# A segmented attention block: the second K product by column halves, half sums of token rows on GpSimd, and a new order of the work

## The chip, the cores and the metric

The kernel runs on one core of a Trainium2 chip. The metric is the device time of one execution in microseconds (us). The kernel before took 807.91 us, the median of three runs (808.39, 807.91 and 807.34).

## The reference

The input x has 2048 tokens of 512 columns. They are cut into 64 segments of 32 tokens, and the segments form a chain: the first eight output rows of one segment, its memory rows, stand ahead of the tokens of the next.

```
h = x + attention(layernorm(x));  out = h + mlp(layernorm(h))

attention: 32 heads of width 128
mem = mem0                                   # 8 rows
for s in range(64):
    h = concatenate([mem, x[32*s : 32*s+32]])   # 40 rows
    q, k, v = h @ Wq, h @ Wk, h @ Wv            # 512 -> 32 heads x 128
    p = softmax(where(mask, q k^T * scale, -1e9))
    o = (p v) @ Wo
    mem = o[:8];  outs.append(o[8:])
mask: a memory row sees all 40 rows; a token sees the memory, itself and the tokens before it
mlp: layernorm, 512 -> 1792, gelu, 1792 -> 512, with biases
```

All weights are bf16. Two layernorms follow one another ahead of the mlp.

## The kernel before

**Packs.** A segment's eight memory rows are on the chain; its tokens are not. The kernel works on 32 rows at a time: pack A of segment s holds its 8 memory rows and 24 of its token rows (tile hT, a ring of slots). The other 8 token rows of four segments are pack B of a block (tile hB), worked one block ahead. There are 16 blocks `bk` of four segments; `sg` = s % 4 is the place of a segment in its block.

**Passes.** A product of a pack with half of WK, WQ or WV (16 heads, 2048 columns) is four passes, one per 128 rows of the weights (`passes` L857, `one_pass` L880). A pass is four matmuls side by side in the columns of TensorE, each 128 rows by 32 columns, streaming 512 columns of weights. `hT` is the stationary operand. A matmul whose stationary operand is still loaded may leave out the load (L605); others load it (L872). K0, K1, Q0, Q1, V0 and V1 are the six products of pack A. Those of pack B, four passes each, fill gaps and are called F0 and F1: eight F passes in each segment of blocks 1 to 14. In sg 3 they are instead the WO product of pack B.

**One segment on TensorE.** Its order is written by hand in ORDERS (L37), one list for each sg: the passes of Q and K, then SC0 (scores of the memory rows and of pack B's rows for heads 0 to 15, L1037, 16 matmuls), V passes and F passes with SC1 (heads 16 to 31) among them, PV0 (probabilities times V of the first half, L1075 and L1080), PVA (L1143, token rows of the segment before), one F pass, the first quarter of WO (L1171, 16 matmuls), PV1, the rest of WO (48 matmuls), SA (scores of pack A's token rows, L1105), and F passes. The next segment then waits for the memory rows in hT.

**The other engines.** The chain of a segment passes through them. K and Q: ScalarE (ACT) or VectorE (DVE) copies the product out of PSUM (L890, L891 with the scale, into tile kq), DVE turns it (L913, into KALL and QT), and GpSimd (POOL) spreads the queries (L927, into ZC). Scores: DVE takes the maximum (L1045, nmc), ACT two exponentials (L1054, EC with its sum smc), DVE for each a reciprocal (L1059, rsc) and a normalized copy (L1062, PC), then one turning (L1064, PTC) that PV waits for. Result: ACT copies PV's output (L890, OT; OTm0 and OTm1 below are its memory rows of PV0 and PV1), WO follows, DVE turns its whole result (L1183, TT), and adds its two halves for the memory rows (L1177, hT, two adds). For the token rows DVE adds the halves likewise (L1177, opT, two adds of 64x96), in its own time. V is copied by ACT (L890, VS; VS0 and VS1 for the halves). GpSimd makes the probabilities of token rows (L1126, PA; turned by DVE L1128) and spreads them (L1132, BD) for PVA, and folds pack B's WO result (L1223 to L1227). The attention's result of a block is turned back by a transposing DMA (`nat`, L1239) and added to x.

**What sets the order.** All operations are recorded with the tiles that they read and write. A planner (`schedule`, L236) then places those that aren't TensorE's: a table PLAN (L43) gives each kind a time within its segment, HOME (L100) the engine where several can do it; an operation goes into the first gap on its engine's line that is free at its earliest time. BANK (L42) gives each product its PSUM bank. Waits on semaphores follow from reads and writes. The order of each engine's queue is fixed by this when the program is built.

After the attention, the mlp runs in its own phase.

## Time and profile before

| what | value |
|---|---|
| median of three runs | 807.91 us |
| span of the profiled execution | 805.9 us (2.05 less than that median) |
| TensorE (PE) busy | 775.0 us, 96% |
| VectorE (DVE) busy | 621.0 us, 77% |
| ScalarE (ACT) busy | 527.1 us, 65% |
| GpSimd (POOL) busy | 349.6 us, 43% |
| a block of four segments, in the middle | 41.14 us |

A row of the timeline gives the start of an instruction (or of several alike) in us from the start of the span, its length in us, its engine, its line in the kernel, the operation, output and inputs by the program's names, shapes and a count. Brackets show idle time ahead of it and what ended that. PEld is TensorE's load of weights, which overlaps the matmuls. TensorE's ends are modelled, so a distance is read from start to start. A row of the waits gives the engine and line that waited, what it waited for, the total in us, the times, and the longest.

### The profile page before, as it was taken

The page shows a single profiled execution, that of the slowest core. Times are in us where ns is not written, and L with a number is a line of the kernel's source. Part 1 is how long each engine was busy: PE and PEld are TensorE (multiplying, and loading weights), DVE is VectorE, ACT ScalarE, POOL GpSimd, SP SyncE. Part 2 cuts the span into 40 slices and gives each one's busy share as a digit, 9 for nine tenths or more (in the row PEclk, how much of TensorE's full clock was granted, in tenths as well). Part 3 has the DMA queues.
Part 4 walks back from the last instruction along what each step waited for, and adds up shares of the span by engine and source line. Part 5 has one row for each costly group of instructions (what it writes and reads, how often), then busy time and mean ns, then how long its engine had stood idle before and what let it go on. Part 6 is the DMA issues. An engine that isn't in the chain of part 4 may idle for free.

```text
span 805.9 us, 43594 instructions
## 1 busy us (share of the span) xinstructions
PE 775.0 (96%) x19308; PEld 422.5 (52%) x18891; DVE 621.0 (77%) x2008; ACT 527.1 (65%) x1522; POOL 349.6 (43%) x886
## 2 busy tenths in 40 slices
...
DMA packets 65449, 48.03 MB, mean 60 GB/s; under 512 B 29028, under 2 KB 61676, under 8 KB 65260
## 3 DMA queue, kind: packets, MB, share of 16 engines
...
q10 hardware_dynamic: 332, 0.27, 0.1%
...
## 4 chain that ended last, share of the span: by engine, by line
PE 91%; DVE 3%; DMA 2%; SPq 2%; ACT 1%; issue 1%; POOL 0%
PE ps L872 43%; PE ps L1171 16%; PE ps L605 6%; PE quad L1579 6%; PE ps L1572 5%; PE ps L1210 4%; PE quad L1075 3%; DMA WQ<-in_A_Wq_dram 2%; SPq L775 2%; PE ps L1105 2%; PE quad L1037 2%; PE ps L1365 2%; PE quad L1143 1%; PE quad L1080 1%; DVE PC L1062 1%; ACT kq L890 1%
## 5 line engine op out<-in xcount | busy, mean ns | idle before, releaser
L872 PE MATMUL ps<-WQ,hT 128*32 128x512 bf16 x2048 | 157.4, 382 | 3.4 <-DVE hT L1177 3.3
L1171 PE MATMUL ps<-WO,OT 128*32 128x256 bf16 x4224 | 140.8, 275 | 1.0 <-ACT OT L890 1.0
L872 PE MATMUL ps<-WV,hT 128*32 128x512 bf16 x1780 | 138.7, 379 | 0.0
L891 ACT ACTIVATE kq<-ps 128x512 bf16<-128x512 f32 x146 | 87.2, 597 | 63.7 <-PE ps L872 63.4
L1126 POOL TENSOR_TENSOR PA<-SA,rsa 128x256 bf16<-128x256 f32 x64 | 39.9, 624 | 183.0 <-DVE rsa L1119 170.6
L890 ACT CAST kq<-ps 128x512 bf16<-128x512 f32 x160 | 93.4, 584 | 38.2 <-PE ps L872 38.2
L1171 PEld LDWEIGHTS ps<-WO,OT 128*32 128x32 bf16 x4224 | 96.2, 97 | 26.5 <-ACT OT L890 12.3
L1132 POOL COPY BD<-PTA 32x192 bf16<-32x192 bf16 x256 | 95.5, 373 | 16.6 <-DVE PTA L1128 0.8
L1062 DVE SCALAR_TENSOR_TENSOR PC<-EC,rsc,even 128x128 bf16<-128x128 f32 x256 | 94.5, 370 | 6.7
L872 PE MATMUL ps<-WK,hT 128*32 128x512 bf16 x1292 | 92.5, 379 | 0.0
L872 PEld LDWEIGHTS ps<-WQ,hT 128*32 128x32 bf16 x2048 | 57.0, 96 | 57.9 <-issue 18.7
L913 DVE STREAM_TRANSPOSE KALL<-kq 128x256 f32<-128x256 f32 x160 | 70.5, 440 | 20.8 <-ACT kq L890 18.6
L1054 ACT ACTIVATE EC<-quad,nmc 128x64 f32<-128x64 f32 x252 | 77.1, 311 | 5.9 <-DVE nmc L1045 0.2
L605 PE MATMUL ps<-WK,hT 128*32 128x512 bf16 x756 | 74.6, 379 | 0.0
L890 ACT CAST VS<-ps 128x512 bf16<-128x512 f32 x126 | 73.7, 585 | 0.7
L890 ACT CAST OT<-quad 128x128 bf16<-128x128 f32 (+1 forms) x205 | 66.3, 363 | 7.5 <-PE quad L1080 5.7
L913 DVE STREAM_TRANSPOSE QT<-kq 128x256 f32<-128x256 f32 x128 | 57.0, 445 | 15.5 <-ACT kq L891 14.1
L872 PEld LDWEIGHTS ps<-WV,hT 128*32 128x32 bf16 x1780 | 50.5, 96 | 34.2 <-issue 1.0
L1575 ACT ACTIVATE WQ<-ps,b1t 128x512 bf16<-128x512 f32 x42 | 28.9, 688 | 52.0 <-PE ps L1572 52.0
L872 PEld LDWEIGHTS ps<-WK,hT 128*32 128x32 bf16 x1292 | 36.4, 97 | 46.1 <-issue 20.1
L1117 ACT ACTIVATE SA<-SA 128x256 f32<-128x256 f32 x64 | 26.7, 417 | 49.4 <-DVE SA L1116 45.0
L1223 POOL TENSOR_TENSOR opT<-TTB,TTS 32x64 bf16<-32x64 f32 x128 | 40.3, 315 | 31.7 <-DVE opT L1177 22.5
...
## 6 DMA issues: line engine op xcount, KB each, us to landing
...
```

The lines of the kernel that those rows point to most:

```text
L605: return e.add_instruction(mybir.InstMatmult(name="I-%d" % (4000000 + _kept[0]), engine=mybir.EngineType.PE, start_tensor_calc=start, stop ...
L872: ins = e.matmul(o, l, m, start=(k == 0), stop=(k == DC - 1), tile_position=(0, 32 * j), skip_group_check=True)
L890: return {"act": (lambda e: e.copy(out, src), t_act(n, ps_)), "dve": (lambda e: e.tensor_copy(out, src), 0.155 + 1.0e-3 * n * fast)}
L891: return {"act": (lambda e: e.mul(out, src, scale_), t_act(n, ps_)), "dve": (lambda e: e.tensor_scalar(out, src, scale_, None, ALU.mult), ...
L913: S.op("dve", lambda e: e.transpose(out, src), reads=[("kq", i)], writes=[key], dur=t_dve(256) + 0.02)
L1054: return e.activation(EC[:, r, sl, :], o[:, sl, :], ACTF.Exp, bias=nmc[:, r, sl:sl + 1], accum_out=smc[:, r, sl:sl + 1])
L1062: S.op("dve", lambda e, sl=sl, xc=xc: e.scalar_tensor_tensor(PC[:, r, :, :, sl], xc, rsc[:, r, sl:sl + 1], ev, ALU.mult, ALU.mult), reads= ...
L1132: S.narrow(S.op("pool", lambda e, j=j, rows=rows: e.tensor_copy(BD[rows, par, :, j, :, :], PTA[rows, :, 0:NA, :]), reads=["PTA"], writes=[ ...
L1171: ins = e.matmul(ps[bank][32 * j:32 * j + 32, 0:256], lhs(slot(h)), wo_cols(h, b), start=(k == 0), stop=(k == 15), tile_position=(0, 32 * ...
L1223: return e.tensor_tensor(o[32 * q:32 * q + 32, c:c + 2], x, y, ALU.add)
L1572: ins = e.matmul(ps[bank][:, 0:SBT], W1[:, cc, fc * P:(fc + 1) * P], hnT_of(k)[:, cc, :], start=(cc == 0), stop=(cc == DC - 1))
L1579: S.op("pe", lambda e: e.matmul(quad[:, t, :], gT_of(k, fc)[:, t * P:(t + 1) * P], W2[:, fc, :], start=(fc == 0), stop=(fc == FC - 1)), re ...
```

## The change

**K1 by column halves.** For every segment but the first, the second K product is done in two halves of its columns, each into a bank of its own (K1 and KX): eight half passes of four matmuls with 256 columns. Their sequence is KSEQ, pairs of half and weight row block; the first half is whole after six of the eight. Each half has its own copy (kql, then kq), its own turning (KAl, then KA, 128x128), its own group of scores (SC1 of 8 matmuls, and SC2), its own prefill of the mask, and its own maximum (nmc, nmd). The exponentials wait for their own maximum.

**Token rows' half sums.** Flag OPA moves the two opT adds from DVE to GpSimd: a copy of the lower halves of TT (opS, 64x192), then two adds (64x96). `nat` waits for both.

**WO's result.** The new code can turn and add it in two halves (TT2); the flag is off, so it is turned and added whole.

**Order.** ORDERS, BANK, PLAN and HOME are new; PLAN has a number for each sg. The planner keeps planned operations on an engine in the order in which they come to it (`placed`). K0 comes ahead of Q0, and pairs of K and Q passes share a loaded operand (3228 matmuls use a kept load, 1024 before). The flags PVM, NRM and P3 are off.

TensorE in segment 37 (sg 1), from the first scores to PV0. L1037 are the scores, `WV,hT` V passes, `WQ,hB` F passes, L1075 PV0. Before:

```order
L1037 MATMUL quad<-KALL,ZC 32x64 x16
L872 MATMUL ps<-WV,hT 32x512 x4
L605 MATMUL ps<-WV,hT 32x512 x4
L872 MATMUL ps<-WV,hT 32x512 x12
L872 MATMUL ps<-WQ,hB 32x512 x4
L1037 MATMUL quad<-KALL,ZC 32x64 x16
L872 MATMUL ps<-WQ,hB 32x512 x4
L872 MATMUL ps<-WV,hT 32x512 x12
L872 MATMUL ps<-WQ,hB 32x512 x4
L1075 MATMUL quad<-PTC,VS 128x2x16 x8
```

The same place now, from the second V pass on (ahead of it stand the 16 matmuls of SC0 and one V pass); L1107 are the scores, L913 and L638 the passes, L1216 PV0:

```order
L638 MATMUL banks<-WV,hT 32x512 x4
L913 MATMUL banks<-WV,hT 32x512 x4
L638 MATMUL banks<-WV,hT 32x512 x4
L1107 MATMUL banks<-KALL,ZC 32x64 x8
L913 MATMUL banks<-WQ,hB 32x512 x4
L913 MATMUL banks<-WV,hT 32x512 x4
L638 MATMUL banks<-WV,hT 32x512 x4
L1107 MATMUL banks<-KALL,ZC 32x64 x8
L913 MATMUL banks<-WV,hT 32x512 x4
L638 MATMUL banks<-WV,hT 32x512 x4
L913 MATMUL banks<-WQ,hB 32x512 x12
L1216 MATMUL banks<-PTC,VS 128x2x16 x8
```

SC1 stood behind six passes; now its first half stands behind four and its second half behind seven. Four F passes stand ahead of PV0 instead of three; behind WO there are three instead of four. In the other sg three F passes stand ahead of PV0 as before, all of them behind SC2.

DVE in segment 39 (sg 3), from the turning of Q1 to the second softmax's turning. L1045 are the maxima, L1059 the reciprocals, L1062 the normalized copies, L1064 the turnings. Before:

```order
L913 STREAM_TRANSPOSE QT<-kq 128x256
L1045 TENSOR_REDUCE nmc<-quad 128x2
L913 STREAM_TRANSPOSE KALL<-kq 128x256
L1059 RECIPROCAL rsc<-smc 128x1
L1062 SCALAR_TENSOR_TENSOR PC<-EC,rsc,even 128x128
L1059 RECIPROCAL rsc<-smc 128x1
L1045 TENSOR_REDUCE nmc<-quad 128x2
L1062 SCALAR_TENSOR_TENSOR PC<-EC,rsc,even 128x128
L1064 STREAM_TRANSPOSE PTC<-PC 128x128
```

Now (L1118 is the whole maximum, L1124 the half ones, PC0 and PTC0 belong to the first softmax, PC1 and PTC1 to the second):

```order
L973 STREAM_TRANSPOSE QT<-kq 128x256
L1118 TENSOR_REDUCE nmc<-banks 128x2
L987 STREAM_TRANSPOSE KALL<-kq 128x4x32 x2
L1124 TENSOR_REDUCE nmc<-banks 128x1
L1156 RECIPROCAL rsc<-smc 128x1 x2
L1159 SCALAR_TENSOR_TENSOR PC0<-EC,rsc,even 128x128 x2
L1156 RECIPROCAL rsc<-smc 128x1
L1124 TENSOR_REDUCE nmc<-banks 128x1
L1161 STREAM_TRANSPOSE PTC0<-PC0 128x128
L1159 SCALAR_TENSOR_TENSOR PC1<-EC,rsc,even 128x128
L1156 RECIPROCAL rsc<-smc 128x1
```

Ahead of PTC0 there are now two half turnings for one whole one, and two half maxima for one whole one; in this sg a reciprocal of the second softmax stands there too. In sg 0 and 2 one reciprocal precedes the half maximum, in sg 0 the other half maximum stands between the two PCs, and in sg 2 the turning of PA stands between the two half turnings.

ACT in segment 38 (sg 2), from the first exponential to the copy of PV0's memory rows (`OT`). Before:

```order
L1054 ACTIVATE EC,smc<-quad,nmc 128x64 [waits sem_dve]
L1054 ACTIVATE EC,smc<-quad,nmc 128x64
L890 CAST VS<-ps 128x512 [waits sem_pe]
L1054 ACTIVATE EC,smc<-quad,nmc 128x64 [waits sem_dve]
L1054 ACTIVATE EC,smc<-quad,nmc 128x64
L890 CAST VS<-ps 128x512 [waits sem_pe]
L890 CAST OT<-quad 128x2x8x8 [waits sem_pe]
```

Now:

```order
L1127 ACTIVATE EC,smc<-banks,nmc 128x64 [waits sem_dve]
L1127 ACTIVATE EC,smc<-banks,nmc 128x64
L1127 ACTIVATE EC,smc<-banks,nmc 128x64 [waits sem_dve]
L950 CAST VS<-banks 128x512 [waits sem_pe]
L1127 ACTIVATE EC,smc<-banks,nmc 128x64 [waits sem_dve]
L950 CAST OT<-banks 128x2x8x8 [waits sem_pe]
L950 CAST VS<-banks 128x512
```

The second V copy stood ahead of the copy of PV0's rows and stands behind it now.

The diff, cut to its core (of ORDERS the list of sg 1, of PLAN two lines):

```diff
-PHASE = (0, 64, 128, 192)
+PHASE = (113, 177, 241, 49)
+TT2, SPL, KCOL, PVM, NRM, P3 = False, True, True, False, 0, False
+OPA = True
+AHEAD = 2.1
+KSEQ = ((0, 0), (1, 0), (1, 1), (0, 1), (0, 2), (0, 3), (1, 3), (1, 2))
...
-          (('Q0', 0, 1), ('K0', 0, 1), ('Q0', 1, 2), ('K0', 1, 2), ('Q0', 2, 3), ('Q1', 0, 1), ('Q0', 3, 4), ('K0', 2, 4), ('Q1', 1, 4), ('K1', 0, 4), ('SC0', 0, 99), ('V0', 0, 1), ('V1', 0, 1), ('V0', 1, 4), ('F1', 0, 1), ('SC1', 0, 99), ('F1', 1, 2), ('V1', 1, 4), ('F1', 2, 3), ('PV0', 0, 99), ('PVA', 0, 99), ('F1', 3, 4), ('WO', 0, 2), ('PV1', 0, 99), ('WO', 2, 8), ('SA', 0, 99), ('F0', 0, 4)),
+          (('K0', 0, 1), ('Q0', 0, 2), ('K0', 1, 2), ('Q0', 2, 3), ('K0', 2, 3), ('Q0', 3, 4), ('K0', 3, 4), ('Q1', 0, 2), ('K1', 0, 1), ('Q1', 2, 4), ('K1', 1, 8), ('SC0', 0, 99), ('V1', 0, 1), ('V0', 0, 2), ('V1', 1, 2), ('SC1', 0, 99), ('F1', 0, 1), ('V1', 2, 3), ('V0', 2, 3), ('SC2', 0, 99), ('V0', 3, 4), ('V1', 3, 4), ('F0', 0, 1), ('F1', 1, 3), ('PV0', 0, 99), ('PVA', 0, 99), ('F1', 3, 4), ('WO', 0, 2), ('PV1', 0, 99), ('WO', 2, 8), ('F0', 1, 3), ('SA', 0, 99), ('F0', 3, 4)),
...
-        "PTC0": (5.74,) * 4,
+        "PTC0": (5.468, 5.559, 5.632, 5.541),
-        "VS1": (6.72,) * 4,
+        "VS1": (7.186, 7.51, 6.962, 7.039),
...
+            fixed = planned(o) is not None
...
-                i = bisect.bisect_right(ST, t)
+                i = max(bisect.bisect_right(ST, t), placed[eng] + 1 if fixed else 0)
...
+        def half_passes(lhs, reads, slot, W, key, r, banks):
+            for n, (h, cc) in enumerate(KSEQ):
+                pad = [0, False]
+                ks = [c for g, c in KSEQ if g == h]
...
+                    for j in range(4):
+                        w = W[:, cc, r * 2048:(r + 1) * 2048].rearrange("p (a y b e) -> p y a b e", a=4, y=2, b=2)[:, h, :, :, 32 * j:32 * j + 32]
+                        o, l, m = ps[banks[h]][32 * j:32 * j + 32, 0:256], lhs(cc), w
...
         def k_seg(s, r, bank):
             par, a0 = s % 2, (s % 2) * HP + 8 * r
+            if r == 1 and SPL and s > 0:
+                for h, (a, b) in enumerate((("kql", "KAl"), ("kq", "KA"))):
...
+                    S.either(copy2(half, v, 256), reads=[("ps", bh)], writes=[(a, r)])
...
-        def sc_softmax(s, r, bank):
+        def sc_softmax(s, r, banks):
...
+                if not whole:
+                    S.op("dve", lambda e, sl=sl, o=o: e.tensor_reduce(nmc[:, r, sl:sl + 1], o[:, sl, :], AX.X, ALU.max, negate=True), reads=[bkey], writes=[("nmd" if sl else "nmc", r)], dur=0.22)
...
+                x = S.op("act", ex, reads=[("nmc" if whole or sl == 0 else "nmd", r)] + [bkey] * (sl or not whole), writes=[ek, sk], dur=0.37)
...
+                    if OPA:
+                        v = TTSX[64:128].rearrange("p c q t -> p (c q t)")[:, 0:2 * DC * NA].rearrange("p (c q t) -> p c q t", c=DC, q=2)
+                        S.narrow(S.op("pool", lambda e: e.tensor_copy(v, tt[0:64, :, :, 0:NA]), reads=[("TTl", par)] * TT2 + [("TT", par)], writes=["opS"], dur=0.35, after=after))
+                        for q2 in range(2):
+                            S.narrow(S.op("pool", lambda e, q2=q2: e.tensor_tensor(o[64 * q2:64 * q2 + 64], tt[64:128, :, q2, 0:NA], v[:, :, q2], ALU.add),
+                                          reads=["opS", ("TT", par)] + [("TTl", par)] * TT2, writes=[("opA%d" % q2, (sx // 4) % 2, sx % 4)], dur=0.4, after=after))
...
+                    if name == "SC1" and SPL and s > 0:
+                        for n_, half in (("SC1", 0), ("SC2", 1)):
...
+                            sc_mm(s, 1, bank_of[n_], half)
...
```

426 lines of the change are left out of this document (286 added, 140 removed), and 4 rows, old and new, of the table ORDERS.

## The prediction

> **What bounds the kernel now.** I read the page's head first, then the windows by block of four segments, the waits by what ended last, and the timelines of one segment. Engines are named as in the profile.
>
> ```profile
> span 805.9 us, 43594 instructions
> PE 775.0 (96%) x19308; PEld 422.5 (52%) x18891; DVE 621.0 (77%) x2008; ACT 527.1 (65%) x1522; POOL 349.6 (43%) x886
> ```
> ```profile
> 410.90:452.04 41.14, 41.14 (x1172) 23.03 (x1117) 37.08 (x124) 30.08 (x91) 20.22 (x52) 1.00 0.13 29
> ```
>
> The span is 805.9 and the median of the runs 807.9, so 2.05 us lie around the span. PE looks full: busy for all of the 41.14 us of a block (10.285 a segment), at the full granted clock. But its ends are modelled and matmuls overlap. The waits (engine, line, what it waited for: total us, times, longest) show that it does wait:
>
> ```profile
> PEld L870 <- DVE hT L1177: 24.8, 62, 1.3
> PEld quad L1075 <- DVE PTC L1064: 12.8, 58, 0.8
> PEld ps L1171 <- ACT OT L890: 12.3, 62, 0.3
> ```
>
> Each of some 62 segments has three places where PE's next weights wait: PV0 (L1075, for PTC), WO (L1171, for the OT copy) and the next segment's first pass (L870, for hT). PE's timeline of segment 38 (start, length) shows the steps; the last two rows are segment 37's first scores and PV0.
>
> ```profile
> 432.47 0.41 PE L872 MATMUL ps<-WQ,hT 128*32 128x512 bf16 x4
> 435.28 0.83 PE L872 MATMUL ps<-WK,hT 128*32 128x512 bf16 x12
> 435.93 0.30 PE L1037 MATMUL quad<-KALL,ZC 128*32 128x64 bf16 x16
> 437.34 0.30 PE L1037 MATMUL quad<-KALL,ZC 128*32 128x64 bf16 x16
> 438.33 0.40 PE L872 MATMUL ps<-WV,hB 128*32 128x512 bf16 x4
> 438.67 0.27 PE L1075 MATMUL quad<-PTC,VS 64*128 64x32 bf16 x8
> 438.84 0.37 PE L1143 MATMUL quad<-BD,VS 64*128 64x48 bf16 x16
> 439.13 0.40 PE L872 MATMUL ps<-WV,hB 128*32 128x512 bf16 x4
> 439.43 0.62 PE L1171 MATMUL ps<-WO,OT 128*32 128x256 bf16 x16
> 439.98 0.27 PE L1075 MATMUL quad<-PTC,VS 64*128 64x32 bf16 x8
> 440.24 1.49 PE L1171 MATMUL ps<-WO,OT 128*32 128x256 bf16 x48
> 441.56 0.42 PE L1105 MATMUL ps<-KALL,QT 128*32 128x32 bf16 x32
> 442.73 0.41 PE L872 MATMUL ps<-WQ,hT 128*32 128x512 bf16 x4
> ```
> ```profile
> 425.60 0.30 PE L1037 MATMUL quad<-KALL,ZC 128*32 128x64 bf16 x16
> 428.37 0.26 PE L1075 MATMUL quad<-PTC,VS 64*128 64x32 bf16 x8
> ```
>
> A pass of four matmuls costs 0.217 (three from 435.28 to 435.93). The segment is 3.46 to SC0, 2.74 from SC0 to PV0, 0.76 to WO, 2.13 to SA, 1.17 from SA to the next pass. Below, times "after SC0" count from 435.93. Between SC0 and PV0 PE has eleven passes, 2.39, and two groups of scores, 0.25: 2.64. The other 0.10 is a bubble ahead of PV0.
>
> **The change, part by part.**
>
> K1 in halves. WO's matmuls have 256 columns too; four of them take 1.32/12 = 0.110 (48 from 440.24 to 441.56); eight half passes are 0.88 against 4 x 0.217 = 0.87. That is +0.015 a segment, x63 = **+1.0**.
>
> SC0 to PV0. DVE's timeline says what sets it now:
>
> ```profile
> 436.31 0.29 DVE L1045 TENSOR_REDUCE nmc<-quad 128x2 f32<-128x128 f32 x1
> 436.77 0.45 DVE L913 STREAM_TRANSPOSE KALL<-kq 128x256 f32<-128x256 f32 x1 [0.17 <-ACT kq L890]
> 437.14 0.12 DVE L1059 RECIPROCAL rsc<-smc 128x1 f32<-128x1 f32 x1
> 437.30 0.38 DVE L1062 SCALAR_TENSOR_TENSOR PC<-EC,rsc,even 128x128 bf16<-128x128 f32 x1
> 437.59 0.15 DVE L1059 RECIPROCAL rsc<-smc 128x1 f32<-128x1 f32 x1
> 437.70 0.29 DVE L1045 TENSOR_REDUCE nmc<-quad 128x2 f32<-128x128 f32 x1
> 437.91 0.35 DVE L1062 SCALAR_TENSOR_TENSOR PC<-EC,rsc,even 128x128 bf16<-128x128 f32 x1
> 438.30 0.31 DVE L1064 STREAM_TRANSPOSE PTC<-PC 128x128 f32<-128x128 f32 x1
> ```
>
> PTC starts 2.37 after SC0, ends at 2.68, and PV0 starts at 2.74. Steps from start to start: maximum 0.21, reciprocal to PC 0.16, PC to reciprocal 0.29, reciprocal to the next 0.11, PC to its PTC 0.39. The second maximum comes 0.36 after its scores' first matmul.
>
> Now SC1 stands after four passes, at 0.125 + 0.87 = 0.99, and has half the matmuls (0.06 less): its maximum can start at 0.99 + 0.30 = 1.30. A half maximum reads 64 columns fewer; I estimate its step at 0.15 (the turnings, 0.45 for 256 columns and 0.31 for 128, give 0.07 for 64), with 0.21 as the upper bound. The two half turnings end ahead of 1.30: they are 0.23 each from 0.59 on.
> - sg 3 (order: maximum, two reciprocals, two PCs, a reciprocal of the second softmax, the other maximum, PTC): 1.30 + 0.15 + 0.11 + 0.16 + 0.29 + 0.29 + 0.11 + 0.15 = 2.56, so PV0 at 2.93, **+0.19**; at the bound +0.31.
> - sg 0 (maximum, reciprocal, PC, other maximum, PC, PTC): 1.30 + 0.15 + 0.11 + 0.29 + 0.15 + 0.39 = 2.39, PV0 at 2.76: +0.01, at the bound +0.13. sg 2, where the turning of PA stands among them, gives 2.38: the same.
> - sg 1 has a fourth F pass ahead of PV0: twelve passes, 2.60 + 0.25 + 0.10 = 2.95 against 428.37 - 425.60 = 2.77 now, **+0.18**; its softmax (2.82) is early enough. The F pass that is gone behind WO saves nothing, since the 1.17 there are the latency of TT and hT.
>
> Sum: 16 x 0.19 + 14 x 0.18 + 31 x 0.01 = **+5.8**; with the bound 16 x 0.31 + 14 x 0.18 + 31 x 0.13 = +11.5. Least of all, only sg 1's pass, +2.5.
>
> ACT's order. Two V copies and OTm0, and the OT copy of PV1:
>
> ```profile
> 438.62 0.58 ACT L890 CAST VS<-ps 128x512 bf16<-128x512 f32 x1
> 439.09 0.29 ACT L890 CAST OT<-quad 128x128 bf16<-128x128 f32 x1
> ...
> 440.35 0.27 ACT L890 CAST OT<-quad 128x128 bf16<-128x128 f32 x1 [0.18 <-PE quad L1080]
> ```
>
> OTm0 starts 0.42 behind PV0 because the V copy, begun 0.05 ahead of it, holds ACT. PV1's copy, with ACT idle, starts 0.37 behind and is 0.02 shorter. With VS1 behind OTm0, WO can start 0.05 to 0.06 earlier. PE's own work there is 0.17 for PV0, 0.29 for PVA and 0.22 for the F pass (starts 438.67, 438.84, 439.13), 0.68 in all, so its floor allows that. I take -0.045 x 62 = **-2.8**. The cover of VS1 is thin: it ends about 1.18 after PV0 and PV1 needs it at 1.31 (439.98 - 438.67); past that, WO's second part waits.
>
> Token rows on GpSimd. DVE loses two opT adds; they stood off the path, so this is worth nothing by itself. GpSimd gains a copy (64x192) and two adds. GpSimd, 43% busy, has room for them. The copy waits for TT, as the hT adds of the turn do, so they run together:
>
> ```profile
> 442.27 0.39 DVE L1177 TENSOR_TENSOR hT<-TT 64x32 bf16<-64x32 f32 x2
> ```
> ```profile
> 651.08 0.85 DVE L1177 TENSOR_TENSOR opT<-TT 64x96 bf16<-64x96 f32 x2
> ```
> ```profile
> 651.13 0.68 POOL L1126 TENSOR_TENSOR PA<-SA,rsa 128x256 bf16<-128x256 f32 x1 [0.34 <-DVE rsa L1119]
> ```
> ```profile
> L1177 DVE TENSOR_TENSOR opT<-TT x128: 252/255/582, 73.1 to 716.0; 64x96 bf16<-64x96 f32 x128
> ```
> ```profile
> L1177 DVE TENSOR_TENSOR hT<-TT x126: 186/189/310, 51.2 to 690.8; 64x32 bf16<-64x32 f32 x126
> ```
> ```profile
> L1225 POOL COPY TTS<-TTB 64x256 f32<-64x256 f32 x32 | 12.6, 393 | 36.2 <-DVE opT L1177 34.4 <-DVE TTB L1214 0.9
> ```
>
> The tile rows give least/median/most in ns. Where a GpSimd instruction began 0.05 behind a pair of opT adds, the pair took 0.85: the second add was 582 ns against 255 and ended about 0.11 behind the GpSimd one. hT adds are 189 at the median and 310 at most. The copy is 0.29 to 0.39 (from L1225, 64x256); I take 0.345, starting 0.05 behind the first add. If the second add then ends 0.05 behind the copy, the pair takes 0.445 against 0.39: +0.055 x 62 = **+3.4**. Bounds: nothing, if the copy doesn't hold it, and +0.19 a segment, if the second add starts only after the copy.
>
> The Trainium skill ("SBUF — State Buffer", section "Who interferes with whom") says that a VectorE instruction with two SBUF inputs contends with a GpSimd instruction that reads SBUF, and that the one issued first makes the other wait in full. The 582 ns row agrees; read strictly it is the +0.19 of that bound, and the sum would be 8.4 higher.
>
> ```profile
> L872 PE MATMUL ps<-WK,hT 128*32 128x512 bf16 x1292 | 92.5, 379 | 0.0
> ...
> L605 PE MATMUL ps<-WK,hT 128*32 128x512 bf16 x756 | 74.6, 379 | 0.0
> ```
>
> The WO result was summed whole before too (one TT): 0. K0 ahead of Q0 waits for the same hT: 0. More kept weights turn L872's matmuls into L605's, which the page's groups give the same mean, 379 ns: 0, and no row has a gain or a loss there.
>
> **Sum**: +1.0 + 5.8 - 2.8 + 3.4 = +7.4: a span of 813.3, and 815.3 with the 2.05 around it.
>
> **The rivals.**
> - *A strict lock of the turn.* The second hT add waits for the whole GpSimd copy: 11.8 in the place of 3.4, **823.7**. For it: the 582 ns. Against: the copy comes second, behind the first add, and most hT adds, with GpSimd at work in some segments, are 186 to 189.
> - *The maxima cost their full step.* DVE's line ahead of PTC0 becomes the bound in sg 0 and 2 too: 11.5 in the place of 5.8, **821.0**. For it: the fixed part of a reduction may be most of its 0.29. Against: the turnings' rows.
> - *Faster: the bubble ahead of PV0 is a wait.* Then PV0 falls towards PE's 2.64 in sg 0, 2 and 3. It decides from a half maximum that hides behind its neighbours (a step below 0.05; sg 0's PTC0 then starts by 2.2), with the reciprocals in sg 3 hidden as well: -0.11 x 46 = -5.1, with ACT's order at its full -3.7, +1.0 for K1, +2.5 for sg 1 and no lock: -5.3, **802.6**. For it: PTC ends just 0.06 ahead of PV0 now, the wait view names PTC 58 times, and SC1 comes 0.4 earlier, which takes the second maximum out of the wait for its scores. Against: PE changes its tile shape there, and PV1 has such a bubble too (439.43 to 439.98 is 0.55 for 0.44 of work).
> - *Costs and gains cancel.* sg 3's late reciprocal and the lock cost nothing, leaving +1.0, +2.5 and -2.8: **808.6**. For it: nothing of either was seen in its own place.
>
> **How the numbers follow.** Forecast 0.38, strict lock 0.09, full maxima 0.11, faster 0.27, cancelling 0.15. The forecast's own range is 811 to 819, by half of each unknown. A measurement of this kernel tells about 0.2% from no change, 1.6 us: faster is below 806.3, slower above 809.5. Faster: 0.25 of its rival, 0.02 of the cancelling and 0.01 of the forecast, 0.28. Same: 0.11 of the cancelling, 0.02 of the faster, 0.03 of the forecast, 0.16. Slower: the rest, 0.56. The range goes from the faster rival's 802.6, which leaves half of it out, 0.13, to 821.5, which leaves out most of the strict lock: 802.5 to 821.5.
>
> **What would show it.** In the profile after: SC0 to PV0 at 2.76, 2.95, 2.75 and 2.93 in sg 0 to 3; PTC0's start in sg 3 about 2.56 after SC0; OTm0 0.37 behind PV0 and WO 0.71 behind it; the pair of hT adds at 0.445 with GpSimd's copy beside it; K1 at 0.88. I'm wrong if PV0 comes earlier than 2.70 anywhere, if hT adds stay at 0.39, or if the turn from WO to the next pass is shorter than now, which no row here promises.

## The result, and the profile after

The changed kernel takes **821.89 us** (median of four runs, 820.89 to 823.20) against 807.75 of the kernel before in the same four rounds (807.34 to 808.39): a ratio of 1.0174, interval 1.0159 to 1.0190. It is slower, as forecast, but by 14.1 us where 7.4 were forecast, and 0.4 us above the top of the range. The span of the profiled execution is 820.2, 14.3 longer.

The page's head after the change (engine, busy us, share, instructions):

```profile
span 820.2 us, 44370 instructions
PE 781.4 (95%) x20320; PEld 407.9 (50%) x18202; DVE 625.0 (76%) x2073; ACT 523.4 (64%) x1580; POOL 416.7 (51%) x1078
```

The window of one block, segments 36 to 39 from SC0 to SC0: its length, then busy us and instructions of PE, PEld, DVE, ACT and POOL, granted clock, DMA share, GB/s.

```profile
423.87:465.84 41.97, 41.76 (x1260) 21.93 (x1067) 37.80 (x130) 29.77 (x95) 24.59 (x65) 1.00 0.11 29
```

DVE lost two adds a segment and has the same share as before (37.80 of 41.97, 37.08 of 41.14), since half turnings and half maxima came. The clock is full in both kernels. So the time is in waits. The rows of the view of waits that concern PV and WO (L1216 is PV, L1319 WO):

```profile
PEld banks L1216 <- ACT VS L950: 27.4, 91, 1.1
PEld banks L1216 <- DVE PTC L1161: 12.5, 18, 1.4
PEld banks L1216 <- DVE rsc L1156: 11.8, 19, 1.4
PEld banks L1319 <- ACT OT L950: 1.2, 6, 0.2
```

Two things are to be seen. WO's wait for the OT copy, 12.3 before, is nearly gone (1.2): the copy comes early enough now. And PV's loads, which wait 51.6 us in all (46.3 before), now have 27.4 of that put down to the V copy on ACT. In the kernel before, nearly all of it was put down to DVE, with 12.8 for PTC and this row:

```profile
PEld quad L1075 <- DVE rsc L1059: 31.6, 64, 0.9
```

The view names the engine whose signal came last, so where the V copy and PTC end together the row tells only one of them.

PE's timeline of segment 37 (sg 1) gives the steps of one segment. L1107 is SC0, L1216 PV0 and PV1, L1291 PVA, L1319 WO, and the last row is the first pass of segment 38:

```profile
434.18 0.30 PE L1107 MATMUL banks<-KALL,ZC 128*32 128x64 bf16 x16
...
437.12 0.27 PE L1216 MATMUL banks<-PTC,VS 64*128 64x32 bf16 x8
...
437.33 0.37 PE L1291 MATMUL banks<-BD,VS 64*128 64x48 bf16 x16
437.63 0.40 PE L913 MATMUL banks<-WQ,hB 128*32 128x512 bf16 x4
437.86 0.61 PE L1319 MATMUL banks<-WO,OT 128*32 128x256 bf16 x16
438.40 0.27 PE L1216 MATMUL banks<-PTC,VS 64*128 64x32 bf16 x8
...
441.21 0.40 PE L913 MATMUL banks<-WK,hT 128*32 128x512 bf16 x4
```

PV0 comes 2.94 after SC0. PVA comes 0.21 behind PV0, where it was 0.17 (438.67 to 438.84), and WO 0.74 behind.

I took these distances, start to start, from both PE timelines. The means in us by sg (0, 1, 2, 3) are those of segments 4 to 59; then come the sums of the differences (after minus before) in these 56 segments and in the three at each end (1 to 3, 60 to 62), and the forecast for all 62:

| stage | before | after | segments 4 to 59 | six at the ends | forecast |
|---|---|---|---|---|---|
| first pass to SC0 | 3.46, 3.46, 3.46, 3.49 | 3.47, 3.47, 3.47, 3.47 | +0.2 | +0.1 | +1.0 |
| SC0 to PV0 | 2.75, 2.77, 2.75, 2.75 | 2.72, 2.95, 2.73, 2.94 | +4.3 | +2.0 | +5.8 |
| PV0 to WO | 0.76, 0.76, 0.76, 0.75 | 0.73, 0.74, 0.79, 0.75 | -0.1 | 0.0 | -2.8 |
| WO to PV1 | 0.55, 0.55, 0.55, 0.55 | 0.56, 0.54, 0.54, 0.63 | +0.9 | +0.5 | 0 |
| PV1 to the end of WO | 1.58, 1.58, 1.58, 1.58 | 1.59, 1.58, 1.58, 1.58 | 0.0 | +2.1 | 0 |
| end of WO to next pass | 1.20, 1.22, 1.18, 1.17 | 1.24, 1.26, 1.27, 1.24 | +3.3 | +0.2 | +3.4 |

Together that is +13.6: 8.7 in segments 4 to 59 and 4.8 in the six at the ends (segment 1 alone +2.1, segment 60 +1.4). Another 0.4 stands ahead of the first pass of segment 1 (SC0 of segment 0 comes 1.1 later, 39.99 instead of 38.88, and segment 0 makes up 0.7 of it), and 0.3 behind the first pass of segment 63.

**The turn.** DVE in segment 37, the turning TT and the pair of hT adds, and GpSimd beside it:

```profile
440.21 0.45 DVE L1333 STREAM_TRANSPOSE TT<-banks 128x256 f32<-128x256 f32 x1
440.69 0.45 DVE L1325 TENSOR_TENSOR hT<-TT 64x32 bf16<-64x32 f32 x2
```
```profile
440.73 0.36 POOL L1348 COPY TTS<-TT 64x192 f32<-64x192 f32 x1
```

The pair takes 0.45 and ends 0.05 behind the copy: 440.73 + 0.36 = 441.09 against 441.14. Both are the forecast's.

### The profile page after: what moved, and what is told of

The parts are those of the page before. It is cut to its first block, busy times and chain, and to the rows that moved or that the text cites. A ratio compares the mean times of both kernels' runs of the same rounds, so it can differ in the third digit from the quotient of the medians.

```text
span 820.2 us, 44370 instructions
## 1 busy us (share of the span) xinstructions
PE 781.4 (95%) x20320; PEld 407.9 (50%) x18202; DVE 625.0 (76%) x2073; ACT 523.4 (64%) x1580; POOL 416.7 (51%) x1078
## 4 chain that ended last, share of the span: by engine, by line
PE 87%; DVE 6%; DMA 2%; SPq 2%; ACT 1%; issue 1%; POOL 0%
PE banks L913 28%; PE banks L638 16%; PE banks L1319 15%; PE banks L1761 6%; PE banks L1754 4%; PE banks L933 3%; PE banks L1216 3%; PE banks L1369 2%; DVE PC L1159 2%; DMA WQ<-in_A_Wq_dram 2%; SPq L813 2%; PE banks L1253 2%; PE banks L1291 2%; PE banks L1107 2%; PE banks L1524 2%; PE banks L1221 1%
## 5 line engine op out<-in xcount | busy, mean ns | idle before, releaser
L1319 PE MATMUL banks<-WO,OT 128*32 128x256 bf16 x4224 | 141.3, 276 | 0.5
L913 PE MATMUL banks<-WQ,hT 128*32 128x512 bf16 x1356 | 112.7, 382 | 0.0
L638 PE MATMUL banks<-WK,hT 128*32 128x512 bf16 x1512 | 111.1, 313 | 0.0
L1319 PEld LDWEIGHTS banks<-WO,OT 128*32 128x32 bf16 x4224 | 100.1, 97 | 18.6 <-issue 1.3
L951 ACT ACTIVATE kq<-banks 128x512 bf16<-128x512 f32 x132 | 78.8, 597 | 41.5 <-PE banks L913 39.3
L638 PE MATMUL banks<-WV,hT 128*32 128x512 bf16 x1024 | 101.0, 378 | 0.4 <-issue 0.4
L913 PE MATMUL banks<-WV,hT 128*32 128x512 bf16 x1024 | 101.1, 379 | 0.0
L950 ACT CAST kq<-banks 128x256 bf16<-128x256 f32 (+1 forms) x209 | 89.0, 457 | 18.7 <-PE banks L913 15.9
L950 ACT CAST OT<-banks 128x128 bf16<-128x128 f32 (+1 forms) x192 | 64.7, 337 | 44.2 <-PE banks L1221 43.9
L1127 ACT ACTIVATE EC<-banks,nmc 128x64 f32<-128x64 f32 x256 | 79.4, 314 | 11.8 <-DVE nmc L1118 3.2
L950 ACT CAST VS<-banks 128x512 bf16<-128x512 f32 x126 | 74.2, 589 | 5.8 <-PE banks L913 4.2
L913 PEld LDWEIGHTS banks<-WQ,hT 128*32 128x32 bf16 x1356 | 38.0, 97 | 72.4 <-issue 53.5
L1274 POOL TENSOR_TENSOR PA<-SA,rsa 128x256 bf16<-128x256 f32 x64 | 39.8, 622 | 62.3 <-DVE rsa L1267 59.8
L638 PE MATMUL banks<-WQ,hT 128*32 128x512 bf16 x692 | 68.2, 379 | 0.0
L1107 PEld LDWEIGHTS banks<-KALL,ZC 128*32 128x32 bf16 x2048 | 41.2, 96 | 50.7 <-DVE KALL L987 23.5
```

The lines of the kernel that those rows point to most:

```text
L638: return e.add_instruction(mybir.InstMatmult(name="I-%d" % (4000000 + _kept[0]), engine=mybir.EngineType.PE, start_tensor_calc=start, stop ...
L913: ins = e.matmul(o, l, m, start=(k == 0), stop=(k == DC - 1), tile_position=(0, 32 * j), skip_group_check=True)
L950: return {"act": (lambda e: e.copy(out, src), t_act(n, ps_)), "dve": (lambda e: e.tensor_copy(out, src), 0.155 + 1.0e-3 * n * fast)}
L951: return {"act": (lambda e: e.mul(out, src, scale_), t_act(n, ps_)), "dve": (lambda e: e.tensor_scalar(out, src, scale_, None, ALU.mult), ...
L1107: ins = e.matmul(o[32 * j:32 * j + 32, sl, :], ZC[:, par, h, :], rhs, start=False, stop=(i == heads[-1]), tile_position=(0, 32 * j), skip_ ...
L1127: return e.activation(EC[:, r, sl, :], o[:, sl, :], ACTF.Exp, bias=nmc[:, r, sl:sl + 1], accum_out=smc[:, r, sl:sl + 1])
```

## The experiments

The theory after the result: the terms for SC0 to PV0 and for the turn are as worked out; ACT's gain is lost because PVA has a new wait; the rest is something that the sum didn't have, above all in the first and last segments. The rivals are named at each experiment. Ratios stand against the kernel before, run beside each; the changed kernel's own is 1.0174. No experiment leaves out any of the computation.

### The turn: GpSimd's copy behind the hT adds

```diff
-reads=[("TTl", par)] * TT2 + [("TT", par)], writes=["opS"]
+reads=[("TTl", par)] * TT2 + [("TT", par)] + [("hTm", (s + 1) % RING)] * mem, writes=["opS"]
```

> The changed kernel with GpSimd's copy of TT made to wait for the two hT adds of the turn. Theory A (the copy beside the adds makes the pair 0.445 instead of 0.39): the pair is 0.39 again, the turn from WO's end to the next pass 0.05 shorter in each segment, 62 x 0.05: 3 to 3.5 us faster than the changed kernel. Theory B (GpSimd has no room for the delay of 0.4 us): its later work (PA, BD) comes late, PVA waits, and nothing or less is won.

820.38 us, ratio 1.0146 (1.0125 to 1.0167). The same adds in segment 37, on DVE, and the copy on GpSimd:

```profile
437.50 0.39 DVE L1325 TENSOR_TENSOR hT<-TT 64x32 bf16<-64x32 f32 x2
```
```profile
438.25 0.34 POOL L1348 COPY TTS<-TT 64x192 f32<-64x192 f32 x1
```

The pair is back at 0.39, and the stage from the end of WO to the next pass is 0.05 to 0.06 shorter in sg 1 to 3 (1.203, 1.211 and 1.190 in the mean of segments 4 to 59), 2.7 us over segments 1 to 62. The intervals of the two ratios overlap, so the time alone would not prove it; the stage does. The copy beside the adds is the cause of most of that term.

### sg 3: the reciprocal and the order on DVE

```diff
-"Ea0": (4.713, 4.771, 4.67, 4.541),
+"Ea0": (4.713, 4.771, 4.67, 4.3),
-"ra1": (6.507, 5.564, 5.693, 5.409),
+"ra1": (6.507, 5.564, 5.693, 5.6),
```

Ea0 is the first softmax's exponential, ra1 the second softmax's reciprocal: in sg 3 the two PCs come earlier and that reciprocal leaves the line ahead of PTC0.

> The changed kernel with two numbers of PLAN changed, so that in sg 3 DVE takes the first reciprocal ahead of the second scores' maximum, and the second softmax's first reciprocal behind PTC0; nothing else moves. Theory A (sg 3's PV0 is late by DVE's order): PV0 in sg 3 goes from 2.94 after SC0 to 2.72 to 2.76, 15 or 16 segments x 0.18 to 0.21: 2.7 to 3.4 us faster. Theory B (PV1 is the later wait in sg 3, since its PTC ends late): PV0 comes earlier, but PV1 moves less than that, and under 1.5 us are gained.

817.85 us, ratio 1.0115 (1.0100 to 1.0130). PE in segment 39, SC0 and PV0:

```profile
452.03 0.30 PE L1107 MATMUL banks<-KALL,ZC 128*32 128x64 bf16 x16
...
454.75 0.21 PE L1216 MATMUL banks<-PTC,VS 64*128 64x32 bf16 x4
```

SC0 to PV0 in sg 3 goes from 2.94 to 2.72. Some is given back between PV0 and WO (+0.07) and won again ahead of PV1 (-0.09): -3.4 us over all segments of sg 3. DVE's order in sg 3 was what held PV0 there, as the sum said.

Both edits at once (the copy behind the adds, and this one):

> The changed kernel with the edits of the third and eighth run together (sg 3's reciprocals as in sg 0, GpSimd's copy behind the two hT adds). Theory A (both terms stand by themselves): the gains add, 3.3 and 3 us, 6 to 7 us faster than the changed kernel, about 815. Theory B (one hides the other, PV1 or the turn taking the place of what is removed): under 4.5 us.

815.55 us, ratio 1.0092 (1.0076 to 1.0109): 6.6 us less than the changed kernel by the ratios, where the two edits alone give 4.8 and 2.3. The two gains add, within the noise. Not stage by stage, though: with both edits the turn is 1.7 us shorter in the profile, and not 2.7.

### sg 1: is it the fourth F pass?

Rival to the sum: PV0 in sg 1 waits for V0's copy, which in this order comes late, since V0's last pass is the fifth-last ahead of PV0. In the changed kernel's segment 37 the load of PV0, the V copy on ACT and PTC0 on DVE are:

```profile
437.11 0.17 PEld L1216 LDWEIGHTS banks<-PTC,VS 64*128 64x128 bf16 x8 [0.42 <-ACT VS L950]
```
```profile
436.38 0.59 ACT L950 CAST VS<-banks 128x512 bf16<-128x512 f32 x1 [0.25 <-PE banks L913]
```
```profile
436.66 0.31 DVE L1161 STREAM_TRANSPOSE PTC<-PC 128x128 f32<-128x128 f32 x1
```

Both end at 436.97, 0.14 ahead of the load. The first experiment takes the fourth F pass to the place behind WO:

```diff
-('V1', 3, 4), ('F0', 0, 1), ('F1', 1, 3), ('PV0', 0, 99), ... ('WO', 2, 8), ('F0', 1, 3),
+('V1', 3, 4), ('F1', 1, 3), ('PV0', 0, 99), ... ('WO', 2, 8), ('F0', 0, 3),
```

> The changed kernel with sg 1's fourth F pass back behind WO. Theory A (that pass alone sets PV0 in sg 1): PV0 comes when its softmax is ready, 2.84 to 2.86 after SC0 instead of 2.95, and nothing is lost behind WO: 14 segments x 0.09 to 0.11, 1.2 to 1.6 us faster. Theory B (the pass fills a gap that is there anyway): PV0 in sg 1 stays at 2.94, the time is the same; or the gap behind WO shrinks no more and it gets longer.

819.74 us, ratio 1.0157 (1.0136 to 1.0179). SC0 to PV0 in sg 1 stays at 2.94. The pass's time has become a wait of the same load (0.61 of idle time in brackets, where it was 0.42):

```profile
439.81 0.20 PEld L1216 LDWEIGHTS banks<-PTC,VS 64*128 64x128 bf16 x8 [0.61 <-ACT VS L950]
```

So the number 2.95 was right and its reason wrong. The second experiment keeps three F passes ahead of PV0, all behind SC2, and puts V0 whole ahead of V1's end:

```diff
-('V1', 0, 1), ('V0', 0, 2), ('V1', 1, 2), ('SC1', 0, 99), ('F1', 0, 1), ('V1', 2, 3), ('V0', 2, 3), ('SC2', 0, 99), ('V0', 3, 4), ('V1', 3, 4), ('F0', 0, 1), ('F1', 1, 3), ('PV0', 0, 99)
+('V0', 0, 1), ('V1', 0, 1), ('V0', 1, 3), ('SC1', 0, 99), ('V0', 3, 4), ('V1', 1, 2), ('SC2', 0, 99), ('V1', 2, 4), ('F1', 0, 3), ('PV0', 0, 99)
```

> The changed kernel with sg 1's order alone changed: three F passes ahead of PV0 instead of four, none of them between the scores, and V0's passes ahead of V1's, so that V0's copy ends about 0.5 us earlier. Theory A (in the second run PV0 in sg 1 stayed at 2.94 since the V copy came as late as PTC0): PV0 in sg 1 at 2.80 to 2.86 after SC0, 14 to 16 segments x 0.1: 1.3 to 2 us faster than the changed kernel. Theory B (PTC0 alone sets it): 2.94 again.

820.55 us, ratio 1.0161 (1.0142 to 1.0180). PV0 comes at 2.85, PV1 0.61 behind WO instead of 0.54. The loads of PV0 and PV1, and what they wait for on ACT (the two V copies) and DVE (the two PTC):

```profile
435.13 0.17 PEld L1216 LDWEIGHTS banks<-PTC,VS 64*128 64x128 bf16 x8 [0.55 <-DVE rsc L1156]
...
436.45 0.19 PEld L1216 LDWEIGHTS banks<-PTC,VS 64*128 64x128 bf16 x8 [0.25 <-ACT VS L950]
```
```profile
434.14 0.58 ACT L950 CAST VS<-banks 128x512 bf16<-128x512 f32 x1
...
435.67 0.59 ACT L950 CAST VS<-banks 128x512 bf16<-128x512 f32 x1
```
```profile
434.77 0.31 DVE L1161 STREAM_TRANSPOSE PTC<-PC 128x128 f32<-128x128 f32 x1
...
436.02 0.31 DVE L1161 STREAM_TRANSPOSE PTC<-PC 128x128 f32<-128x128 f32 x1
```

PV0's V copy ends 0.4 ahead of the load (434.72), PTC0 at 435.08, as long behind SC0 as before (2.79), and the load starts 0.05 behind it. For PV1 both end late (436.26 and 436.33), and the load starts 0.12 behind the later one. This difference returns below. V0's copy, ending together with PTC0, is shown to hold PV0 in sg 1 by some 0.09; the gain is mostly lost again at PV1, since V1's passes are now the late ones.

### ACT's order: where the 2.8 went

First, the order alone, in the kernel before: OTm0 ahead of VS1. The OT copies of the token rows are planned later and on ACT, so that they don't come between.

```diff
-S.either(copy2(ot, src, 128), reads=CQ, writes=[("OTm", par, r)])
+x, v = S.either(copy2(ot, src, 128), reads=CQ, writes=[("OTm", par, r)]), S.last_writer[("VS", s % 3, 1)]; v.prev = x if r == 0 < s else v.prev
-"OTx0": (7.22, 7.22, 7.71, 7.22), "OTx1": (7.71, 8.1, 8.1, 7.71),
+"OTx0": (8.6,) * 4, "OTx1": (8.7,) * 4,
```

> The kernel before with the copy of PV0's memory rows ahead of the second V copy on ACT, and the copies of token rows behind PV1's copy. Theory A (in the kernel before that V copy is all that holds WO; in the changed kernel PVA, which waits for the last exponential's bank, holds it instead): WO starts 0.69 to 0.71 after PV0 instead of 0.755 in all sg, 62 x 0.05: about 3 us faster than the kernel before, 804.7. Theory B (something else starts WO at 0.75, or the V copy is then late for PV1): WO or PV1 stays where it is, and the time is within 1 us of the kernel before or longer.

809.98 us, ratio 1.0013 (1.0004 to 1.0023). WO comes 0.69 behind PV0 instead of 0.755, 3.2 us over all, so PE's floor does allow it, in the kernel before. But PV1 comes 0.65 behind WO instead of 0.55, which costs 5.2. Loads of PV0, WO and PV1 in segment 38, and the ends that PV1 needs:

```profile
440.49 0.17 PEld L1075 LDWEIGHTS quad<-PTC,VS 64*128 64x128 bf16 x8 [0.45 <-DVE rsc L1059]
...
441.19 0.34 PEld L1171 LDWEIGHTS ps<-WO,OT 128*32 128x32 bf16 x16
441.81 0.20 PEld L1075 LDWEIGHTS quad<-PTC,VS 64*128 64x128 bf16 x8 [0.28 <-ACT VS L890]
```
```profile
441.03 0.59 ACT L890 CAST VS<-ps 128x512 bf16<-128x512 f32 x1
```
```profile
441.38 0.31 DVE L1064 STREAM_TRANSPOSE PTC<-PC 128x128 f32<-128x128 f32 x1
```

The V copy ends at 441.62 and the turning at 441.69, about where PV1 stood before; the load starts 0.12 behind the later. The cover that the prediction called thin is gone by a way that it didn't name: not the copy's length but a wait for two late ends.

Second, in the changed kernel: does PVA wait for the last exponential of SC2, which reads bank 3, where PVA writes? In the kernel before, in segment 38, the last exponential ends at 438.64, 0.03 ahead of PV0:

```profile
438.33 0.31 ACT L1054 ACTIVATE EC<-quad,nmc 128x64 f32<-128x64 f32 x1
```

In the changed kernel's segment 37 ACT's rows are:

```profile
436.87 0.32 ACT L1127 ACTIVATE EC<-banks,nmc 128x64 f32<-128x64 f32 x1
437.07 0.20 ACT L1127 ACTIVATION_READ_ACCUMULATOR EC<-banks,nmc 128x1 f32 x1
437.49 0.27 ACT L950 CAST OT<-banks 128x128 bf16<-128x128 f32 x1 [0.21 <-PE banks L1221]
```

It ends at 437.27 with its sum (the second row), 0.15 behind PV0, and PVA starts at 437.33. The OT copy is at 0.37 behind PV0, as forecast, but PE is not ready: PVA 0.21, its own 0.30 and the F pass's 0.23 make 0.74. The experiment puts SC2 in another bank in sg 0 and 2:

```diff
-bank_of = OPEN_BANK if s == 0 else BANK
+bank_of = OPEN_BANK if s == 0 else dict(BANK, SC2=4) if s % 2 == 0 and s > 2 else BANK
```

> The changed kernel with the second half's scores of sg 0 and sg 2 in bank 4 instead of bank 3, in which PVA writes. Theory A (PVA waits until the last exponential has read bank 3; that is why WO won nothing from ACT's order): PVA starts 0.17 to 0.18 behind PV0 in sg 0 instead of 0.205, WO 0.69 to 0.71 behind it instead of 0.735, and sg 2, where BD also is late, wins less: under 1 us in all, so the profile has to tell. Theory B (PVA waits for BD or for TensorE's own change of shape): 0.205 again.

825.53 us, ratio 1.0216 (1.0196 to 1.0236). Segment 36 (sg 0), PV0, PVA and WO on PE, and the exponential on ACT:

```profile
426.70 0.27 PE L1216 MATMUL banks<-PTC,VS 64*128 64x32 bf16 x8
426.86 0.37 PE L1291 MATMUL banks<-BD,VS 64*128 64x48 bf16 x16
427.39 0.29 PE L1319 MATMUL banks<-WO,OT 128*32 128x256 bf16 x4
```
```profile
426.43 0.32 ACT L1127 ACTIVATE EC<-banks,nmc 128x64 f32<-128x64 f32 x1
```

PVA is at 0.16 behind PV0 (0.205 in the changed kernel's sg 0) and WO at 0.69 (0.73), with the exponential ending 0.04 behind PV0, by the median, where it was 0.06. At most 0.02 of the 0.045 can come from that earlier end, and BD ends 0.25 ahead of PV0 in both kernels, so the bank's wait is what held PVA in sg 0. Sg 3, which keeps bank 3, stays at 0.22. In sg 2 PVA also waits for BD from the busier GpSimd, which in the changed kernel ends 0.11 behind PV0 (0.21 ahead of it in the kernel before); there PVA goes from 0.25 to 0.20 behind PV0 although BD ends 0.03 later still. The kernel as a whole got slower: the mask's copy into bank 4, and the turning of PA behind it, now stand in DVE's line ahead of PTC0, and PV0 in sg 0 moves, by the median, from 2.72 to 2.96.

### Two semaphores on one load

What the loads above have in common: PV waits for two engines. Of the two waits one stands on the load itself; the other on an instruction of its own ahead of it in PE's queue (L526 in the kernel before, mostly L556 in the changed one). Which is which follows from the planner's estimate: the end that is expected last goes on the load. In each late case above the extra instruction is the one for PTC. In the changed kernel's segment 37, for instance, PTC0 ends at 436.97, its instruction runs from 437.01 to 437.06, and the load starts at 437.11. Theory: a late end costs about 0.06 when its wait is on the load and about 0.15 when it is on the extra instruction. The rival: the order makes no difference. First the order of all double waits of PE is turned round, in the kernel before, in the edit of ACT's order, and in the changed kernel with three F passes in sg 1:

```diff
-key=lambda p: -(p.start + p.dur + self.lat(p, o))
+key=lambda p: (1 if E == "pe" else -1) * (p.start + p.dur + self.lat(p, o))
```

> The kernel before with the order of double waits on TensorE turned, and nothing else. Theory A: its PV0 has one wait and its PV1 and scores are held by TensorE, so there is nothing to win: within 1 us of the kernel before. Theory B (the order of waits is worth something by itself, everywhere): 2 us or more faster.

> The fourth run's kernel with one more edit: where a TensorE instruction waits for two semaphores, the wait that is expected to end first stands first. Theory A (PV1 came at 1.345 after PV0 there since it waits for both the V copy and PTC1, and the second wait, taken only after the late first one, costs 0.08): PV1 starts 0.06 behind PTC1's end instead of 0.14, at 1.26 to 1.28 after PV0, and the 3 us that WO's early start won are kept: 62 x 0.05 faster than the kernel before, about 805. Theory B (the V copy or TensorE itself is what PV1 waits for): PV1 stays at 1.34, the time is that of the fourth run.

> The second run's kernel (three F passes ahead of PV0 in sg 1) with the order of double waits on TensorE turned. Theory A (PV0 there came 0.15 behind both PTC0 and the V copy, 0.08 of it the second wait): PV0 in sg 1 goes from 2.94 to 2.86 after SC0 and PV1 in sg 3 from 0.64 to 0.56 behind WO: about 16 x 0.08 + 15 x 0.08, 2.5 us less than the second run. Theory B: the distance of 0.15 is the V copy's own latency and stays; no change.

Before: 817.86, ratio 1.0121 (1.0107 to 1.0135). ACT's order: 818.29, 1.0129 (1.0112 to 1.0145). Three F passes: 828.72, 1.0262 (1.0245 to 1.0279). Each is 8 to 10 us slower than the same kernel with its waits as they were. The loss ahead of PV0, in all three, I had not foreseen. In the kernel before with its waits turned, the load of PV0 in segment 37 and the turning that ends last ahead of it:

```profile
434.35 0.19 PEld L1075 LDWEIGHTS quad<-PTC,VS 64*128 64x128 bf16 x8 [0.51 <-ACT EC L1054]
```
```profile
433.92 0.31 DVE L1064 STREAM_TRANSPOSE PTC<-PC 128x128 f32<-128x128 f32 x1
```

The load starts 0.12 behind PTC0's end at 434.23; with the waits as they were, it was 0.05 (438.61 to 438.66, in segment 38). SC0 to PV0 is 2.86 instead of 2.75, 7.2 us in 62 segments. The row also shows a trap: the wait is put down to an exponential that PV doesn't read. The stage behind the end of WO in sg 0 got longer too (1.22 to 1.48); why is open. With the waits turned, PV1 in the edit of ACT's order came earlier (0.58 behind WO instead of 0.65), which is what theory said of that place. In the edit with three F passes PV1 in sg 3 came at 0.54 behind WO, as hoped, but PV0 in sg 1 at 3.00, where 2.86 was hoped for: PTC0 and the V copy end together there, so in either order one of the two ends is on the extra instruction, and both ended 0.06 later than with the waits as they were.

So the wait for PTC, on PV only, is put on the load, in the edit of ACT's order on the kernel before:

```diff
-key=lambda p: -(p.start + p.dur + self.lat(p, o))
+key=lambda p: (o.mode != MH or p.eng != "dve", -(p.start + p.dur + self.lat(p, o)))
```

> The fourth run's kernel (the kernel before, OTm0 ahead of the second V copy on ACT) with the double waits of PV alone set so that PV's weight load itself waits for PTC, and an instruction of its own ahead of it for the V copy; all other double waits as in the fourth run. Theory A (a wait that ends last costs 0.06 on the load and 0.15 on the instruction of its own): PV0 stays at 2.74 to 2.75 after SC0, PV1 comes 1.26 to 1.28 after PV0 instead of 1.34, and WO's 3 us are kept: 804 to 805.5, faster than both kernels. Theory B (PV1 can't come ahead of 1.31 for another reason): 807 to 808.

807.14 us (12 runs) against 808.15 (17 runs): ratio 0.9986, interval 0.9976 to 0.9995. Loads of PV0, WO and PV1 in segment 38:

```profile
437.11 0.17 PEld L1075 LDWEIGHTS quad<-PTC,VS 64*128 64x128 bf16 x8 [0.43 <-DVE rsc L1059]
...
437.80 0.34 PEld L1171 LDWEIGHTS ps<-WO,OT 128*32 128x32 bf16 x16
438.36 0.19 PEld L1075 LDWEIGHTS quad<-PTC,VS 64*128 64x128 bf16 x8 [0.22 <-DVE PTC L1064]
```

PV1 follows PTC1 (437.99 + 0.31 = 438.30 on DVE) by 0.06 instead of 0.12. Against the kernel before, PV0 to WO is 3.4 us shorter over all and WO to PV1 0.8 longer; 1.6 go back in the turn, most of it in sg 1 and 3, where other work of DVE now stands ahead of TT. It beats both kernels, by little.

### The adds back on DVE, and K1 whole

```diff
-OPA = True
+OPA = False
```

> The changed kernel with the flag OPA off: the token rows' half sums are two adds on DVE again; TensorE's and ACT's orders stay. Theory A (GpSimd's copy beside the two hT adds makes the pair 0.445 us instead of 0.39, in every segment): the pair falls back to 0.39, the stretch from WO's end to the next pass gets 0.05 shorter in each of some 62 segments, and in sg 3 PV1 comes sooner too, as GpSimd's adds no longer run beside DVE's PC: 3.5 to 5 us faster than the changed kernel, about 817.5. Theory B (the copy is hidden, DVE's relief was a gain): DVE has 0.5 us more in each segment and the time is the same or up to 3 us longer.

838.98 us, ratio 1.0375 (1.0358 to 1.0393): some 16 us slower than the changed kernel by the ratios. A row of its waits (59.8 in the changed kernel, for the same wait):

```profile
POOL PA L1274 <- DVE rsa L1267: 132.6, 45, 8.3
```

DVE's line is late in many places: the block of segments 36 to 39 takes 42.9 us (41.97 in the changed kernel), and in sg 0 the first pass to SC0 takes 3.97 at the median instead of 3.47. Neither theory had this size. With the new plan DVE has no room for the two adds, so this order needed the move to GpSimd. What the move is worth in the order before, no run shows.

One thing that was expected did come: without GpSimd's adds beside it, DVE's first PC of PV1's half takes 0.32 in sg 3 (0.55 in the changed kernel), and WO to PV1 there is 0.54 at the median instead of 0.64. In segment 39:

```profile
469.27 0.32 DVE L1159 SCALAR_TENSOR_TENSOR PC<-EC,rsc,even 128x128 bf16<-128x128 f32 x1
```

```diff
-TT2, SPL, KCOL, PVM, NRM, P3 = False, True, True, False, 0, False
+TT2, SPL, KCOL, PVM, NRM, P3 = False, False, False, False, 0, False
```

with K1 as four passes, SC1 whole in SC2's place, K1's bank 6, and V0's copy tied to ACT in HOME.

> The changed kernel's orders with the second K product whole again, one group of scores in the place of SC2, and GpSimd's half sums kept. Theory A (the halves themselves are worth and cost little; the loss sits in sg 1, in sg 3 and in the turn): SC0 to PV0 is between 2.72 and 2.80 in sg 0 and 2, the turn keeps GpSimd's 0.055, and the time is within 5 us of the changed kernel on either side. Theory B (the halves are what costs): 8 us or more faster than the changed kernel, near the kernel before.

869.42 us, ratio 1.0757 (1.0737 to 1.0777). This tells nothing about the halves themselves. In the changed kernel V0's copy stands on ACT behind the first exponential of the second softmax, which needs only the half scores of SC1. Without them this exponential comes later, and in sg 1 and 2 the second one stands ahead of V0's copy too; PV waits for that copy:

```profile
PEld banks L1216 <- ACT VS L950: 80.3, 113, 2.2
```

Order and halves belong together; I found no single edit that undoes the halves alone.

### The ends of the chain

The three segments at each end lost 4.8 us (the 4.2 of the expectation counts from SC0 of segment 0, and so takes in what segment 0 makes up). Theory: PLAN's numbers, made for the middle, are bad there. Rival: something else.

```diff
-return PLAN.get(k, (None,) * 4)[o.tag[0] % 4]
+return PLAN.get(k, (None,) * 4)[o.tag[0] % 4] if 4 <= o.tag[0] < 59 else None
```

> The changed kernel with PLAN's numbers used for segments 4 to 58 alone; in the first and last segments the planner goes by its path lengths. Theory A (the numbers fit the middle, where F passes stand, and cost 4.2 us in segments 1 to 3 and 60 to 62): 2 to 4 us faster than the changed kernel. Theory B (those segments are long for other reasons, the halves or the new banks): no change or longer.

826.36 us, ratio 1.0243 (1.0220 to 1.0266): slower, not faster, so the theory falls as it stands. Of the 6.3 us by which the profile is longer than the changed kernel's, 4.2 lie behind the first pass of segment 63, of which the theory said nothing. Of the six end segments segment 1 alone gains clearly, 0.85: its stage from PV1 to the end of WO, 2.59 in the changed kernel, is 1.58 again. Segments 2, 60 and 62 are 0.7, 1.7 and 0.8 longer. So the numbers cost something in segment 1, but to do without them all doesn't bring the 4.8 us back, and most of their cause stays open.

Last, all four places mended at once: the copy behind the adds, sg 3's order, V0 first in sg 1, SC2's bank.

> The changed kernel with four edits together: sg 3's reciprocals, GpSimd's copy behind the hT adds, sg 1's order of the eleventh run, and the bank of the thirteenth. Theory A (the terms add): 6.6 us from the first two, 1.3 from sg 1, 0.5 from the bank: 8 to 9 us faster than the changed kernel, about 813, still slower than the kernel before by some 5 us, which sit in the first and last segments and in sg 1 and 2. Theory B (they overlap): 815 to 816, as with two.

815.93 us, ratio 1.0109 (1.0092 to 1.0126), no better than the two alone (1.0092). The bank's edit puts the mask into DVE's critical line (SC0 to PV0 in sg 0 is 3.2 us longer over all than in the changed kernel), and what sg 1 gains goes into it.

## Why the prediction was right or wrong

- **SC0 to PV0: the places right, the sum in part by luck, +6.3 for +5.8** (its three terms add up to 5.9). The places 2.76, 2.95, 2.75, 2.93 came out as 2.72, 2.95, 2.73, 2.94. In segments 4 to 59 alone the same terms give 5.5, and 4.3 were measured; the other 2.0 lie in the six end segments, for which the sum had no reason of its own. For sg 3 the reason is shown (its order on DVE). For sg 1 the reason was wrong: not the fourth F pass, but V0's copy ending together with PTC0. The sum had looked at the softmax and not at the V copy. In sg 0 and 2 two errors are small against each other: in segment 36 PTC0 starts 2.31 after SC0 (426.18) where 2.39 was worked out, and its end is 0.10 ahead of PV0's load where 0.06 was (the median of sg 2 is 0.14 ahead of PV0).
- **The turn: right, +3.5 for +3.4,** in size and place, shown by the copy behind the adds. The Trainium skill ("SBUF — State Buffer", section "Who interferes with whom"), read strictly, gave 0.19 a segment; the trace shows 0.05 to 0.06.
- **ACT's order: a step that failed, -0.1 for -2.8.** "PE's own work there is 0.17 for PV0, 0.29 for PVA and 0.22 for the F pass, 0.68 in all, so its floor allows that. I take -0.045 x 62 = -2.8." OTm0 did move to 0.37 behind PV0. But PVA writes the bank that SC2's exponential reads, and that exponential now ends after PV0 starts, so PVA stands at 0.21 to 0.25 behind PV0 in place of 0.17, and the work is 0.74 long. The 0.68 was taken from a trace in which that exponential ended 0.03 ahead of PV0.
- **The ends of the chain: the other step that failed, and the larger one.** The prediction took the middle of the chain for the whole: it multiplied terms of one middle segment by 62 and put nothing for the opening and the ends. In segments 4 to 59 its terms give 6.9, and 8.7 were measured. The six end segments cost 4.8 where its terms give 0.5, and 0.7 more stand ahead of segment 1 and in segment 63 and behind it. Of the 4.8, 2.1 lie from PV1 to the end of WO (segments 1, 60 and 61) and 2.0 from SC0 to PV0. Why is open but for segment 1, where PLAN's numbers have a part. Either of the two steps alone would have left the time inside the range (818.0 with ACT's order as measured, 820.3 with the ends); it took both.
- **WO to PV1: not in the sum, +1.4,** of it 0.9 in segments 4 to 59. There it is sg 3, 0.63 for 0.55, about 0.08 a segment. DVE's first PC of PV1's half takes 0.55 where two adds of GpSimd run beside it, so PTC1 is late (459.24), and PV1's load starts 0.12 behind it. DVE in segment 39 (a half maximum and the reciprocal behind it, then the two PCs and PTC1), GpSimd, and the load:

```profile
456.37 0.22 DVE L1124 TENSOR_REDUCE nmc<-banks 128x1 f32<-128x64 f32 x1 [0.21 <-PE banks L1107]
456.51 0.21 DVE L1156 RECIPROCAL rsc<-smc 128x1 f32<-128x1 f32 x2
...
457.88 0.55 DVE L1159 SCALAR_TENSOR_TENSOR PC<-EC,rsc,even 128x128 bf16<-128x128 f32 x1
...
458.52 0.37 DVE L1159 SCALAR_TENSOR_TENSOR PC<-EC,rsc,even 128x128 bf16<-128x128 f32 x1
458.93 0.31 DVE L1161 STREAM_TRANSPOSE PTC<-PC 128x128 f32<-128x128 f32 x1
```
```profile
457.88 0.85 POOL L1350 TENSOR_TENSOR opT<-TT,TTS 64x96 bf16<-64x96 f32 x2
```
```profile
459.36 0.20 PEld L1216 LDWEIGHTS banks<-PTC,VS 64*128 64x128 bf16 x8 [0.28 <-ACT VS L950]
```

  The prediction had GpSimd's copy beside the hT adds, and not its adds beside DVE's other work. The run with the sums on DVE bears it out (PC 0.32, WO to PV1 0.54). But it moved DVE's order too, and no experiment moved these adds alone, so for this place the cause is well supported and not isolated.
- **The rivals.** The half maximum's step is 0.14 (456.37 to 456.51), so not the full 0.21; the pair of adds 0.45, so no strict lock; and nothing cancelled. Of the rival with the bubble the runs decide less: PV0 came nowhere ahead of 2.70, but PTC0 started at 2.31 where the rival asked for 2.2, so whether PV0 follows an earlier PTC0 was not tested. That the bubble is at least in part a wait is seen the other way round: with PE's waits turned in the kernel before, PV0 came 0.11 later. The time lies near the strict lock's 823.7, but not by its mechanism.
- **Token rows on GpSimd: "worth nothing by itself" fails for the new plan,** where some 16 us hang on it. For the order before, no run has it.
- **K1 in halves: +0.3 for +1.0,** small either way; the stage holds the new order of K and Q passes too, and no run parts them.
